# A recurrent attention and feed-forward kernel on one core: the last two tasks' products regrouped by output block, the count of the range check loaded ahead of them

## The chip, the cores and the metric

The kernel runs on one core of a Trainium2 chip. A core has TensorE (PE, matrix products into PSUM), VectorE (DVE), ScalarE (ACT), GpSimd (POOL) and SyncE (SP), each with an instruction queue of its own that runs in order; transfers are issued from the queues of SP, ACT and POOL. The metric is the time of one execution on the device in microseconds, the median of several runs.

## The reference

A recurrent attention (4 batches, 8 heads, 768 steps, head dimension 48) is followed by a feed-forward network with a gelu:

```python
for t in range(S):
    cur = einsum('bhd,bhe->bhde', u * k[t], v[t])
    y[t] = einsum('bhd,bhde->bhe', r[t], state + cur)
    state = w[t][..., None] * state + einsum('bhd,bhe->bhde', k[t], v[t])
h = x @ w_in            # x: y as 3072 tokens x 384; w_in: 384 x 2048
g = h / (1 + exp(-1.702 * h))
out = g @ w_out         # 2048 x 384
```

## The kernel before

**Attention.** The 3072 tokens are cut into 24 chunks of 128 (six chunks per batch, `CB` = 6). chunk(t) turns the recurrence within a chunk into small matmuls with running products of the decay w. load(t) fetches a chunk's inputs from SP's queue. From chunk 6 (`t >= CB`) on, half of the head pairs lie with their two heads swapped between the row halves; so when t is CB, load also fetches the u masks a second time into `hm`, in three transfers: the unswapped half of the pairs (line 169) and the swapped half in two pieces (line 171, `SWAPPED`). The first WHOLE = 8 chunks use these masks in the product `ps_d` (line 326); for a chunk from CB on it takes the second copy for all four pairs.

**Feed-forward.** The chunks form six groups of four. A task (group, first chunk, last chunk, f) does for one block f of 128 hidden units: first_product (9 matmuls x by w_in into `ph`, each value as a high and a low part, so three products per block of inputs, lines 438 to 440), gelu (two ACT operations and one VectorE operation that make the high part `gh` and the low part `gl`, lines 449 to 452) and second_product (for each of the NM = 3 blocks of 128 outputs three matmuls into `po[m]`: woh by gh, wol by gh, woh by gl, lines 465 to 467). There are 106 tasks, numbered 0 to 105; the last 16 are those of the last group, each 512 tokens wide. The three `po` tiles take one PSUM bank each and collect all 16 blocks f. store (lines 470 to 475) scales each `po[m]` on ACT into `ob` and sends it out from SP's queue, 256 KB per block.

**Order.** Everything of both parts is issued inside `tc.manual_schedule()`: the written order holds on each engine. The ramp is a list of tokens (RAMP, such as `l6` for a piece of load(6)); after it rest() yields per step j: first product j (`g`), gelu j (`h`), and second product j - LAG (`y`), LAG = 2, with the pieces of attention between. At the end of the list j runs to 107: the first product and gelu of task 104, the second product of 102, first product and gelu of 105, second products of 103, 104 and 105, and the last store.

**The range check.** While attention and weights pass through, ACT collects sums of squares and of magnitudes in `acc`. At the end (lines 570 to 581, outside the ordered region, where a planner places the operations) VectorE compares them with two limits (line 571) and adds the results (573), TensorE sums over the partitions (575, a product with one column), VectorE casts the sum to an integer in `acc` (577), and every engine loads it into a register (`nc.values_load`, 580). With `tc.If(n < full)` (581) a slow general path would follow if a limit had been passed. With these inputs it does not, so every engine branches over it; line 680 is the program's end.

Of the kernel before, what the change touches and what calls it, by code (L numbers as in the profile page):

```python
# [9 lines left out]
F32 = mybir.dt.float32  # L10
F32R = mybir.dt.float32r
BF16 = mybir.dt.bfloat16
I32 = mybir.dt.int32
U32 = mybir.dt.uint32
AF = mybir.ActivationFunctionType
ALU = mybir.AluOpType
# [78 lines left out]
def rwkv_ffn_kernel(ctx: ExitStack, tc, wkr, vp, vrk, ub, w_in, w_out, masks, vt, uc, out):  # L95
# [59 lines left out]
    def load(t):  # L155

        n = NP * CW + 1
        a, v = wkr_t[t % 2], v_t[t % 3]
        loaded[t] = [a, v]
        if t == 0:  # L160
            nc.sync.dma_start(a[ROWS, 0:n], wkr[t, :, 0:n])
            yield
            A.dma_start(a[ROWS, n:], wkr[t, :, n:])
        elif t < CB:
            nc.sync.dma_start(a[ROWS], wkr[t])
        else:
            if t == CB:
                m = 2 + 2 * HALF
                nc.sync.dma_start(hm[ROWS, 2 + H : H + m], masks[:, 2:m])
                for dst, rows in SWAPPED:  # L170
                    nc.sync.dma_start(hm[dst, H + m :], masks[rows, m:])
            kr, kr_in = (x.rearrange("r (i q c) -> r i q c", i=2, q=2) for x in (a[:, n:], wkr[t, :, n:]))
            cut = 1 + HALF * CW
            nc.sync.dma_start(a[ROWS, 0:cut], wkr[t, :, 0:cut])
            for dst, rows in SWAPPED:
                nc.sync.dma_start(a[dst, cut:n], wkr[t, rows, cut:n])
            nc.sync.dma_start(kr[ROWS, :, 0], kr_in[:, :, 0])
            for dst, rows in SWAPPED:
                nc.sync.dma_start(kr[dst, :, 1], kr_in[rows, :, 1])
        yield  # L180
        nc.sync.dma_start(v[:, OFF:], vrk[t, :, 0:DM])
        if t >= WHOLE:
            rk = pools["late"].tile([P, 2 * DM], F32, tag="rk", name="rk_t")
            nc.sync.dma_start(rk, vrk[t, :, DM:])
            loaded[t].append(rk)
        yield
# [70 lines left out]
    def bank(name):  # L257

        i = free.pop(0)
        x = ps_a.tile([P, WIDE], F32, tag=f"bank{i}", name=name)  # L260
        held[id(x)] = i, x
        while cold:
            for _ in range(cold.pop()):
                T.matmul(x.rearrange("p (n c) -> p n c", c=P), warm, warm_b, start=True, stop=True)
        return x
# [10 lines left out]
    def chunk(t):  # L276
# [45 lines left out]
        if t < WHOLE:  # L322
            got = bank("ps_d")
            ps_d = by_p(got, 2)
            for p in range(NP):
                T.matmul(ps_d[:, p], rk[:, p], u_heads[:, int(t >= CB), p], start=True, stop=True)  # L326
        yield
        if t < WHOLE:
            A.copy(s, got[:, 0:H])
# [125 lines left out]
    def second_product(j, task):  # L455
        i, c0, c1, f = task
        gh, gl = parts.pop(j)
        first = i not in po
        if first:
            po[i] = [ps_o.tile([P, WIDE], F32, tag=f"po{m}", name=f"po{m}") for m in range(NM)]  # L460
        for m in range(NM):
            ms = slice(m * P, (m + 1) * P)
            o = po[i][m][:, c0 * C : c1 * C]

            T.matmul(o, woh[:, f, ms], gh, start=first, stop=False, skip_group_check=True)  # L465
            T.matmul(o, wol[:, f, ms], gh, start=False, stop=False, skip_group_check=True)  # L466
            T.matmul(o, woh[:, f, ms], gl, start=False, stop=f == NF - 1, skip_group_check=True)  # L467

    def store(i, start, N):

        for m, o in enumerate(po.pop(i)):
            ob = pools["late"].tile([P, WIDE], F32, tag="ob", name="ob", bufs=3)[:, 0:N]
            A.activation(ob, o[:, 0:N], AF.Copy, scale=1.0 / W_SCALE)
            nc.sync.dma_start(out[m, :, bass.ds(start, N)], ob)
        xs.pop(i)

    def new_x(i):

        return (mo if i % 2 == 0 else pools["late"]).tile([P, 2, NP, WIDE], F32R, tag="x", name="x", bufs=1)

    with tc.manual_schedule():
        early = ExitStack()
        su = early.enter_context(tc.tile_pool(name="su", bufs=1))
        where = [(i, col) for i, n in enumerate(CHUNKS) for col in range(n)]
        starts = [sum(CHUNKS[:i]) for i in range(len(CHUNKS))]
        last = {}
        for j, task in enumerate(TASKS):
            last[task[0]] = j
        running, told = {}, {}

        def piece(kind, i):

            if (kind, i) not in running:
                running[kind, i] = {
                    "l": load, "a": chunk, "m": measures.get, "w": lambda i: convert(i, su, False)
                }[kind](i)
            next(running[kind, i])

        def do(token):
            kind, i = token[0], int(token[1:] or 0)  # L500
            told[token] = told.get(token, 0) + 1
            if kind in "lamw":
                piece(kind, i)
                if kind == "w" and all(told.get(f"w{n}") == 4 for n in range(2 * NL)):
                    early.close()
                    pools["late"] = fast.enter_context(tc.tile_pool(name="late", bufs=2))

                    pools["late"].tile([P, GAP], F32, tag="gap", name="gap", bufs=1)
            elif kind == "f":
                fetch(i, su)  # L510
            elif kind == "x":
                group, col = where[i]
                if i == 1:
                    fill_x(xs[group], 0, 2 * C)
                elif i == 3:
                    fill_x(xs[group], 2 * C, 4 * C)
                elif col == CHUNKS[group] - 1:
                    fill_x(xs[group], 0, (col + 1) * C)
            elif kind == "d":
                cold.append(i)  # L520
            elif kind == "u":
                nc.sync.dma_start(u_sb, ub)
            elif kind == "M":
                nc.sync.dma_start(hm[ROWS, 0 : 2 + H], masks)
            elif kind == "g":
                first_product(i, TASKS[i])
            elif kind == "h":
                gelu(i, TASKS[i])
            elif kind == "y":
                second_product(i, TASKS[i])  # L530
                group = TASKS[i][0]
                if i == last[group]:
                    store(group, starts[group] * C, CHUNKS[group] * C)

        def rest():

            begins = []
            for t, (i, col) in enumerate(where):
                n = len([x for x in TASKS if x[0] == i - 1])
                begins.append(last.get(i - 1, -1) + 1 - BEFORE - round((CHUNKS[i] - 1 - col) * n / CHUNKS[i]))  # L540
            left = []
            for t, begin in enumerate(begins):
                ramp = dict(told)
                for kind, step, half, rank in PARTS:
                    token = f"{kind}{t + 2 * (kind == 'l')}"
                    if kind == "l" and t + 2 >= NT:
                        continue
                    if ramp.get(token, 0):
                        ramp[token] -= 1
                    else:  # L550
                        left.append((step + begin, half, rank, token))
            left.sort(key=lambda x: x[:3])
            for j in range(FIRST, len(TASKS) + LAG):
                for post in range(3):
                    if post and j < len(TASKS):
                        yield f"{'gh'[post - 1]}{j}"
                    while left and left[0][:2] <= (j, post):
                        yield left.pop(0)[3]
                if j - LAG >= 0 and f"y{j - LAG}" not in told:
                    yield f"y{j - LAG}"  # L560

        for token in RAMP.split():
            do(token)
        for token in rest():
            do(token)
# [1 line left out]

    for x, limit in ((acc[:, 0 : 2 * NT], LIMIT), (acc[:, 2 * NT :], W_MAX)):  # L570
        V.tensor_single_scalar(x, x, limit, op=ALU.is_lt)
    oks = at.tile([P, 1], F32, tag="s", name="oks", bufs=2)
    V.tensor_reduce(oks, acc, axis=AX.X, op=ALU.add)
    ps = bank("ps_n")[0:1, 0:1]
    T.matmul(ps, oks, oks, start=True, stop=True)
    cnt = acc[0:1, 0:1].bitcast(I32)
    V.tensor_copy(cnt, ps)
    fast.close()
    full = P * acc.shape[1] ** 2
    n = nc.values_load(cnt, min_val=0, max_val=full)  # L580
    with tc.If(n < full):
        with tc.tile_pool(name="wp", bufs=2) as wp:
            for i in range(2 * NL):
                fetch(i, wp)
# [100 lines left out]
```

## Time and profile before

| | us |
|---|---|
| median of 3 runs | 511.07 (511.02 to 513.05) |
| profiled execution | 512.25 |
| its span in the trace | 510.5 |

| engine | busy, us | share |
|---|---|---|
| PE (matmul) | 490.8 | 96% |
| PEld (weight load, beside PE) | 407.7 | 80% |
| DVE | 296.8 | 58% |
| ACT | 249.8 | 49% |
| POOL | 13.7 | 3% |

A row of the trace's view in order of time gives start, duration, engine, line, operation, output and inputs with shapes, and in brackets the idle time before it with what ended it. In the view of one line the durations stand as minimum/median/maximum in ns, then the first and last start. SPq, PEldq and so on are instructions of an engine's queue (branches, semaphore waits, register loads, issues of transfers) that do not count as busy. Matmul durations overlap: the distance between starts is what one costs.

### The profile page before, as it was taken

To read this page: it belongs to the slowest core of one execution; us is meant where nothing else is said; L and a number is where in the kernel's file an instruction comes from. 1 tells how busy PE (TensorE), PEld (TensorE's weight loads), DVE (VectorE), ACT (ScalarE), POOL (GpSimd) and SP (SyncE) were. 2 spreads that over 40 slices of the span, in tenths; PEclk is the share of its full clock that TensorE was granted. 3 is DMA by queue.
4 is the path that set the end of the run, shared out by engine and by line. 5 is a ranking of instruction groups with operands and counts; after the bars stand their busy time and mean duration, and the time that the engine had idled before them with its cause. 6 is when DMAs were issued, how large, how long until landed. Compare 5 with 4: busy or idle time off the path is not lost.

```text
span 510.5 us, 11971 instructions
## 1 busy us (share of the span) xinstructions
PE 490.8 (96%) x5065; PEld 407.7 (80%) x5065; DVE 296.8 (58%) x507; ACT 249.8 (49%) x532; POOL 13.7 (3%) x45
## 2 busy tenths in 40 slices
PE   7788999999999999999999999999999999999994
PEld 3567999987888888888888888888888878888883
DVE  8899999787777762656556555555655521111110
ACT  4887989856726453352542543452552432322221
POOL 2010100000100010000001000001000000000000
PEclk9998899999999999999999999999999999999999
DMA  8988665034641532042204062204040001100001
GB/s 211 261 251 233 195 185 158 17 88 133 173 125 31 172 82 60 1 157 63 79 2 121 5 193 83 68 1 125 16 142 1 1 1 31 63 0 2 0 2 68
DMA packets 26830, 45.94 MB, mean 90 GB/s; under 512 B 4096, under 2 KB 17856, under 8 KB 26768
## 3 DMA queue, kind: packets, MB, share of 16 engines
q1 hardware_dynamic: 25984, 43.52, 29.9%
q0 software_dynamic: 672, 1.18, 1.2%
q8 instruction: 42, 0.69, 0.6%
q10 hardware_dynamic: 112, 0.39, 0.2%
q14 instruction: 20, 0.16, 0.1%
HBM read 38.00 MB, written 4.72 MB: 84 GB/s over the span
## 4 chain that ended last, share of the span: by engine, by line
PE 89%; DMA 5%; DVE 3%; ACT 1%; issue 1%; SPq 0%; DVEq 0%; ACTq 0%
PE po L465 14%; PE ph L438 13%; PE po L466 13%; PE po L467 13%; PE ph L439 13%; PE ph L440 13%; DMA wkr_t<-in_wkr 3%; PE ps_y L396 3%; PE ps_y L383 3%; PE ps_u L360 2%; PE ps_u L356 2%; DMA st<-in_w_in 2%; PE ps_t L306 2%; PE ps_d L326 1%; DVE lp L288 0%
## 5 line engine op out<-in xcount | busy, mean ns | idle before, releaser
L452 DVE TENSOR_TENSOR gl<-gf,gh 128x512 fp32r<-128x512 f32 (+1 forms) x106 | 67.9, 641 | 156.6 <-ACT gf L450 155.4
L449 ACT ACTIVATE gh<-ph 128x512 fp32r<-128x512 f32 (+1 forms) x106 | 59.2, 558 | 197.5 <-PE ph L440 177.8
L438 PE MATMUL ph<-x,wih 128*128 128x512 f32 (+1 forms) x318 | 119.8, 377 | 1.4 <-DMA x<-x 1.4
L465 PE MATMUL po<-gh,woh 128*128 128x512 f32 (+1 forms) x318 | 120.6, 379 | 0.0
L466 PE MATMUL po<-gh,wol 128*128 128x512 f32 (+1 forms) x318 | 118.2, 372 | 0.0
L467 PE MATMUL po<-gl,woh 128*128 128x512 f32 (+1 forms) x318 | 118.2, 372 | 0.0
L440 PE MATMUL ph<-x,wil 128*128 128x512 f32 (+1 forms) x318 | 117.4, 369 | 0.0
L439 PE MATMUL ph<-x,wih 128*128 128x512 f32 (+1 forms) x318 | 117.4, 369 | 0.0
L438 PEld LDWEIGHTS ph<-x,wih 128*128 128x128 f32 x318 | 59.9, 188 | 12.2 <-ACT junk L236 1.9
L465 PEld LDWEIGHTS po<-gh,woh 128*128 128x128 f32 x318 | 60.5, 190 | 10.8
L467 PEld LDWEIGHTS po<-gl,woh 128*128 128x128 f32 x318 | 60.6, 190 | 10.5 <-DVE gl L452 0.2
L466 PEld LDWEIGHTS po<-gh,wol 128*128 128x128 f32 x318 | 60.6, 191 | 9.5
L440 PEld LDWEIGHTS ph<-x,wil 128*128 128x128 f32 x318 | 59.9, 188 | 10.3
L439 PEld LDWEIGHTS ph<-x,wih 128*128 128x128 f32 x318 | 60.0, 189 | 9.4
L450 ACT ACTIVATE gf<-ph 128x512 f32<-128x512 f32 (+1 forms) x106 | 58.8, 555 | 2.7 <-DVE gl L452 2.6
L236 ACT ACTIVATE junk<-lp 112x1032 bf16<-112x1032 f32 x24 | 25.6, 1066 | 12.6 <-DVE lp L293 12.6
L299 DVE TENSOR_TENSOR kq<-wkr_t,lp 112x1024 f32<-112x1024 f32 x24 | 29.3, 1222 | 2.6 <-PE ps_y L396 1.6
L288 DVE TENSOR_TENSOR_SCAN lp<-wkr_t,d1r 112x516 f32<-112x516 f32 x24 | 29.4, 1225 | 1.7 <-DMA wkr_t<-in_wkr 1.7
L293 DVE TENSOR_TENSOR_SCAN lp<-wkr_t,d1f 112x516 f32<-112x516 f32 x24 | 29.6, 1231 | 0.7
L396 PE MATMUL ps_y<-kq,mid 64*64 64x64 f32 (+3 forms) x384 | 24.6, 223 | 3.6 <-DVE mid L406 1.4
L236 ACT ACTIVATE junk<-kq 112x1024 bf16<-112x1024 f32 x24 | 25.4, 1059 | 0.2
L396 PEld LDWEIGHTS ps_y<-kq,mid 64*64 64x64 f32 (+3 forms) x384 | 19.6, 130 | 5.6 <-DVE mid L406 2.1
(76 smaller groups left out, 475.1 us busy)
## 6 DMA issues: line engine op xcount, KB each, us to landing
st<-in_w_out SPq DMA_DIRECT2D x6, 1024.0 KB, 7.5
rk_t<-in_vrk SPq DMA_DIRECT2D x16, 384.0 KB, 3.5
st<-in_w_in SPq DMA_DIRECT2D x6, 896.0 KB, 8.4
v_t<-in_vrk SPq DMA_DIRECT2D x24, 192.0 KB, 2.8
out_t<-ob SPq DMA_DIRECT2D x18, 256.0 KB, 2.5
wkr_t<-in_wkr SPq DMA_DIRECT2D x18, 192.0 KB, 2.6
wkr_t<-in_wkr SPq DMA_DIRECT2D x36, 96.0 KB, 2.3
wkr_t<-in_wkr SPq DMA_DIRECT2D x5, 577.9 KB, 5.8
```

The source lines that it names most:

```text
L236: A.activation(junk[:, 0 : x.shape[1]], x, AF.Square, accum_out=acc[0:R2, i : i + 1])
L293: V.tensor_tensor_scan(pm, w0, d1f.rearrange("r p c -> r (p c)"), 0.0, op0=ALU.mult, op1=ALU.add)
L396: T.matmul(ps[b][head(h), p], from_[head(half), p * D + OFF * h : p * D + HB], qf[head(half), p, blocks[b]], start=False, stop=p == PAIRS[ ...
L438: T.matmul(ph, h_, xs[i][:, 0, c, cs], start=c == 0, stop=False)
L439: T.matmul(ph, h_, xs[i][:, 1, c, cs], start=False, stop=False)
L440: T.matmul(ph, l_, xs[i][:, 0, c, cs], start=False, stop=c == NM - 1)
L449: A.activation(gh, ph, AF.Gelu_apprx_sigmoid, scale=1.0 / W_SCALE)
L450: A.activation(gf, ph, AF.Gelu_apprx_sigmoid, scale=1.0 / W_SCALE)
L452: V.tensor_tensor(gl, gf, gh.bitcast(F32), op=ALU.subtract)
L465: T.matmul(o, woh[:, f, ms], gh, start=first, stop=False, skip_group_check=True)
L466: T.matmul(o, wol[:, f, ms], gh, start=False, stop=False, skip_group_check=True)
L467: T.matmul(o, woh[:, f, ms], gl, start=False, stop=f == NF - 1, skip_group_check=True)
```

## The change

Three parts.

1. In load(6) the transfer of the unswapped masks is dropped, and one of the two swapped pieces is issued from POOL's queue instead of SP's. The product `ps_d` takes the second copy for the swapped pairs alone.
2. The check's four operations move from behind the ordered region into it (judge), ahead of the second product of task 102 and behind gelu 104. The register load moves ahead of the last products; the branch stays where it was.
3. The second products of tasks 104 and 105 and the last store become finish(105): block by block, for each m both tasks' three matmuls, then scaling and store. The last block (m = 2) is cut into two halves of 256 tokens: six matmuls, scaling on ACT and a 128 KB store from ACT's queue for the first, six matmuls, scaling on VectorE and a 128 KB store from SP's queue for the second.

```diff
             if t == CB:
                 m = 2 + 2 * HALF
-                nc.sync.dma_start(hm[ROWS, 2 + H : H + m], masks[:, 2:m])
-                for dst, rows in SWAPPED:
-                    nc.sync.dma_start(hm[dst, H + m :], masks[rows, m:])
+                for q, (dst, rows) in zip((G, nc.sync), SWAPPED):
+                    q.dma_start(hm[dst, H + m :], masks[rows, m:])
...
-                T.matmul(ps_d[:, p], rk[:, p], u_heads[:, int(t >= CB), p], start=True, stop=True)
+                T.matmul(ps_d[:, p], rk[:, p], u_heads[:, int(t >= CB and p >= HALF), p], start=True, stop=True)
...
+    def finish(j):
+        i, c0, c1, _ = TASKS[j]
+        start, half = starts[i] * C, (c1 - c0) * C // 2
+        both = [(TASKS[q][3], *parts.pop(q)) for q in (j - 1, j)]
+        for m, o in enumerate(po.pop(i)):
+            ms = slice(m * P, (m + 1) * P)
+            ob = pools["late"].tile([P, WIDE], F32, tag="ob", name="ob", bufs=3)
+            cuts = (0, half, 2 * half) if m == NM - 1 else (0, 2 * half)
+            for n, (a, b) in enumerate(zip(cuts, cuts[1:])):
+                for f, gh, gl in both:
+                    for w, g in ((woh, gh), (wol, gh), (woh, gl)):
+                        done = f == NF - 1 and g is gl
+                        T.matmul(o[:, a:b], w[:, f, ms], g[:, a:b], start=False, stop=done, skip_group_check=True)
+                if n == 0:
+                    A.activation(ob[:, a:b], o[:, a:b], AF.Copy, scale=1.0 / W_SCALE)
+                else:
+                    V.tensor_single_scalar(ob[:, a:b], o[:, a:b], 1.0 / W_SCALE, op=ALU.mult)
+                q = A if m == NM - 1 and n == 0 else nc.sync
+                q.dma_start(out[m, :, start + a : start + b], ob[:, a:b])
...
             elif kind == "y":
-                second_product(i, TASKS[i])
                 group = TASKS[i][0]
-                if i == last[group]:
+                if i == len(TASKS) - 4:
+                    judge()
+                if i == len(TASKS) - 1:
+                    bad.append(nc.values_load(cnt, min_val=0, max_val=full) < full)
+                    finish(i)
+                elif i < len(TASKS) - 2:
+                    second_product(i, TASKS[i])
+                if i == last[group] and i < len(TASKS) - 1:
                     store(group, starts[group] * C, CHUNKS[group] * C)
+
+        def judge():
+            for x, limit in ((acc[:, 0 : 2 * NT], LIMIT), (acc[:, 2 * NT :], W_MAX)):
+                V.tensor_single_scalar(x, x, limit, op=ALU.is_lt)
+            oks = at.tile([P, 1], F32, tag="s", name="oks", bufs=2)
+            V.tensor_reduce(oks, acc, axis=AX.X, op=ALU.add)
+            got = bank("ps_n")
+            ps = got[0:1, 0:1]
+            T.matmul(ps, oks, oks, start=True, stop=True)
+            V.tensor_copy(cnt, ps)
+            release(got)
...
-    for x, limit in ((acc[:, 0 : 2 * NT], LIMIT), (acc[:, 2 * NT :], W_MAX)):
-        V.tensor_single_scalar(x, x, limit, op=ALU.is_lt)
-    oks = at.tile([P, 1], F32, tag="s", name="oks", bufs=2)
-    V.tensor_reduce(oks, acc, axis=AX.X, op=ALU.add)
-    ps = bank("ps_n")[0:1, 0:1]
-    T.matmul(ps, oks, oks, start=True, stop=True)
-    cnt = acc[0:1, 0:1].bitcast(I32)
-    V.tensor_copy(cnt, ps)
     fast.close()
-    full = P * acc.shape[1] ** 2
-    n = nc.values_load(cnt, min_val=0, max_val=full)
-    with tc.If(n < full):
+    with tc.If(bad[0]):
```

More of the change, by code (lines that the diff above doesn't have):

```diff
@@ L475, in store @@
         xs.pop(i)
+    def finish(j):
[17 more added lines that the diff above has]
+                q.dma_start(out[m, :, start + a : start + b], ob[:, a:b])
+        xs.pop(i)
     def new_x(i):
@@ L529, in do @@
             elif kind == "y":
-                second_product(i, TASKS[i])
                 group = TASKS[i][0]
-                if i == last[group]:
-                    store(group, starts[group] * C, CHUNKS[group] * C)
+                if i == len(TASKS) - 4:
[6 more added lines that the diff above has]
+                if i == last[group] and i < len(TASKS) - 1:
+                    store(group, starts[group] * C, CHUNKS[group] * C)
+        def judge():
[8 more added lines that the diff above has]
+            release(got)
+        cnt = acc[0:1, 0:1].bitcast(I32)
+        full = P * acc.shape[1] ** 2
+        bad = []
         def rest():
```

## The prediction

> **What bounds the kernel now.** I read the page's chain first, then the trace in order of time from 490 us on, then the queues' own instructions there.
>
> ```profile
> PE 89%; DMA 5%; DVE 3%; ACT 1%; issue 1%; SPq 0%; DVEq 0%; ACTq 0%
> ```
>
> TensorE carries 89% of the chain that ended last, so whatever stops PE in the last 20 us is paid in full, and so is whatever comes after PE's last matmul. The last tasks, in order of time:
>
> ```profile
> 492.27 0.39 PE L440 MATMUL ph<-x,wil 128*128 128x512 f32 x1
> ...
> 492.72 0.39 PE L466 MATMUL po<-gh,wol 128*128 128x512 f32 x1
> ...
> 493.81 0.69 DVE L452 TENSOR_TENSOR gl<-gf,gh 128x512 fp32r<-128x512 f32 x1 [3.39 <-ACT gf L450]
> ...
> 498.61 0.39 PE L465 MATMUL po<-gh,woh 128*128 128x512 f32 x1
> ...
> 500.74 0.09 PEld L575 LDWEIGHTS ps_n<-oks 128*1 128x1 f32 x2 [0.35 <-issue]
> ...
> 500.87 0.50 PE L465 MATMUL po<-gh,woh 128*128 128x512 f32 x1
> ...
> 501.20 0.39 PE L466 MATMUL po<-gh,wol 128*128 128x512 f32 x1
> ...
> 501.86 1.99 ACT L473 ACTIVATE ob<-po 128x512 f32<-128x512 f32 x3 [4.00 <-PE po L467]
> ...
> 502.82 0.40 PE L467 MATMUL po<-gl,woh 128*128 128x512 f32 x1
> ```
>
> 492.27 is the last matmul of task 104's first product; task 102's second product follows at once (its second matmul at 492.72, so a 512-column matmul every 0.227 us). Task 104's gl is written by VectorE from 493.81 to 494.50. 498.61 opens task 104's second product, 500.87 task 105's. The count's matmul (L575) lies between those two. The third activation ends at 501.86 + 1.99 = 503.85. After that:
>
> ```profile
> 503.24 1.37 SPq L474 DMA_DIRECT2D out_t<-ob  x1
> 504.71 0.37 SPq L474 DMA_DIRECT2D out_t<-ob  x1
> DMA to landing us min/median/max: 3.1/3.1/3.1
> L581 SPq COMPARE_BRANCH  x1: 45/45/45, 505.1 to 505.1; - x1
> L581 SPq EVENT_SEMAPHORE  x8: 17/17/17, 508.3 to 508.9; - x8
> L581 PEldq COMPARE_BRANCH  x1: 3637/3637/3637, 501.9 to 501.9; - x1
> L581 DVEq COMPARE_BRANCH  x1: 72/72/72, 501.8 to 501.8; - x1
> L581 DVEq EVENT_SEMAPHORE  x1: 21/21/21, 504.7 to 504.7; - x1
> ```
>
> The last store is ready at 503.85 but SP issues it at 504.71, because the second store's issue takes 1.37. It lands 3.1 later, at 507.8. SP, which takes the branch over the general path at 505.1, runs its next instruction only at 508.3, half a us after the landing: **SP's jump of about 3.15 sets the end, not the store.** VectorE's jump takes 2.8 (501.9 to 504.7), TensorE's branch 3.64. From 508.3 to the end at 510.5 SP counts off semaphores and the last barrier runs. Why did one issue take 1.37?
>
> ```profile
> q8 instruction: 1, 0.02, 5.9%
> 144.47 1.31 SPq L181 DMA_DIRECT2D v_t<-in_vrk  x1
> q8 instruction: 1, 0.02, 6.2%
> ```
>
> The first row is the DMA view of 502.90 to 504.25: one instruction fetch on q8. The second and third show it elsewhere: an SP issue that began inside such a fetch (window 144.2 to 145.4) lasted until 145.78, 0.38 after that window; in the tail it lasted until 504.61, 0.36 after. The tail's fetch follows TensorE's branch (501.9) by one us. So TensorE's jump holds up an SP issue that falls into its fetch.
>
> **The change, part by part.**
>
> *The count's place.* judge() is issued after task 104's gelu and before task 102's second product, and this region keeps the written order on each engine. VectorE gets its three operations behind gl104, TensorE gets the count's matmul ahead of task 102, and behind that matmul wait all of TensorE's later products. Today the three run early, in holes:
>
> ```profile
> L571 DVE TENSOR_SCALAR acc<-acc x2: 164/172/179, 91.2 to 401.5; 128x12 f32<-128x12 f32 x1, 128x48 f32<-128x48 f32 x1
> L573 DVE TENSOR_REDUCE oks<-acc x1: 203/203/203, 402.0 to 402.0; 128x1 f32<-128x60 f32 x1
> 125.81 0.15 ACT L406 COPY mid<-ps_y 1x1 f32<-1x1 f32 x1 [0.36 <-PE ps_y L396]
> 126.01 0.13 PEld L396 LDWEIGHTS ps_y<-kq,mid 64*64 64x64 f32 x1 [0.42 <-ACT mid L406]
> ```
>
> gl104 ends at 494.50; 0.179 + 0.164 + 0.203 = 0.55 makes 495.05; TensorE wakes 0.05 after the operation it waits for (125.96 to 126.01). From the count's weight load to the second full matmul behind it are 501.20 - 500.74 = 0.46. So task 102's second matmul moves from 492.72 to 495.56: **+2.84**, which nothing hides, since all of TensorE's remaining work is behind it and gelu 105 moves along. On VectorE the count's cast and gl105 are queued behind, but gl105's inputs come later by the same 2.84. Bounds: 2.6 if the VectorE operations overlap, 3.1 with a further gap at each. The stall's cover would be VectorE's idle 3.39 ahead of gl104, but the operations are queued behind gl104, not in it.
>
> *The register load* stands before the last products. TensorE's costs nothing:
>
> ```profile
> L580 PEldq TENSOR_LOAD <-acc x1: 485/485/485, 501.3 to 501.3; - x1
> ```
>
> It ran at 501.3 while matmuls went on until after 502.82: the queue covers its 0.49, and it would cost that if the queue ran dry. ACT, SP and VectorE are idle at its new place.
>
> *The tail, in the old clock (without the 2.84).* The count's matmul is gone from it: task 105's second matmul would come ten pitches after 498.61, at 500.89 instead of 501.20, a gain of 0.32. Blocks 0 and 1 take twelve matmuls, 498.61 to 501.34. Block 2 is twelve matmuls of 256 columns:
>
> ```profile
> 57.92 0.12 PE ph L439
> ...
> 62.00 0.12 PE ph L440
> ...
> L449 ACT ACTIVATE gh<-ph 128x256 fp32r<-128x256 f32 x20 | 7.7, 384 | 1.6 <-PE po L466 1.6
> L406 DVE COPY mid<-ps_y x16: 145/146/147, 144.1 to 418.3; 1x1 f32<-1x1 f32 x16
> L367 DVE TENSOR_TENSOR mid<-ps_u,sf x20: 357/358/359, 19.3 to 401.7; 112x192 f32<-112x192 f32 x20
> ```
>
> 35 such matmuls from 57.92 on keep 0.12, so the halves cost 12 x 0.12 = 1.44 against 1.36. First half: last matmul 501.94. Today 0.43 pass from the last matmul's start to ACT's (502.82 to 503.25), 0.11 less with 256 columns: ACT starts at 502.26, takes 0.38, ends 502.64 and issues its store in the shade. Second half: it writes the same bank (po2) that ACT is reading. Does TensorE wait? No row has just this; the nearest:
>
> ```profile
> 44.67 0.67 PE ps_u L356 x23
> 45.34 0.61 PE ps_u L360 x27
> ...
> 45.98 0.37 DVE mid L367
> ```
>
> L367 reads only what L356 wrote, yet it starts behind L360, which writes other columns of the same bank. So I take it that banks are kept apart as a whole, in the other direction too. Between nothing and 0.75, I take the wait: TensorE resumes at 502.69, loses 0.10 restarting, its sixth matmul is at 503.39, VectorE starts at 503.71. Its operation was never run at this shape; from 0.146 at one element and 0.358 at 192, 256 give 0.43 (bounds 0.33 to 0.5). SP can issue at about 504.15.
>
> [...]
>
> *The issue and the jump.* TensorE sends its last instruction between 502.69 and 503.39 and then branches; its fetch starts one us later and lasts about 1.3, so it covers roughly 503.9 to 505.25. SP's last issue at 504.15 begins inside it and ends 0.37 after it, at 505.6, branch 505.6: **+0.45** against today's 505.14. SP's jump, between 2.8 (VectorE's) and 3.15 (its own), taken in the middle: **-0.18**. The 128 KB landing stays under it (504.71's 256 KB needed 3.1).
>
> *The ramp.*
>
> ```profile
> L169 SPq DMA_DIRECT2D hm<-in_masks x1: 1174/1174/1174, 59.7 to 59.7; - x1
> L171 SPq DMA_DIRECT2D hm<-in_masks x2: 420/424/428, 60.9 to 61.4; - x2
> 110.63 0.47 PE ps_d L326 x5
> ```
>
> SP loses L169 and one L171 (1.17 + 0.42), POOL gains one DMA. The masks are first used by chunk 6's ps_d at 110.6, nearly 50 us later, and TensorE is busy around 60. I take 0 and keep 0.3 both ways.
>
> Sum: 2.84 + 0.45 - 0.18 = +3.1. The profiled execution took 512.25, span 510.5, so 1.7 lie outside the span; its time stands 1.2 above the median 511.07. The sum is a difference of spans and I add it to the median: **514.2**.
>
> **The rivals.**
> 1. *The last issue misses the fetch* (TensorE's branch goes out later or VectorE ends sooner; 0.2 us decide). Issue 504.15 to 504.53, branch 504.59, -0.55: 2.84 - 0.55 - 0.18 = +2.1, **513.2**.
> 2. *No wait on the bank.* The second half runs on at 502.06 to 502.66, VectorE 502.98 to 503.41, SP 503.45 to 503.82, branch 503.86, -1.28: +1.4, **512.5**. For it speaks that the halves share no bytes; against it L367.
> 3. *No stall, not slower.* If VectorE's three operations came ahead of gl104, in its idle 3.39, the sums would be ready before 492.44 and TensorE would not wait. Then only the tail counts: between -1.28 - 0.18 = -1.5 (**509.6**) and +0.3 (**511.3**). For it: the same operations are placed early today. Against: today they stand behind the ordered region, now within it.
> 4. *The clock drops in the stall.*
>
> ```profile
> 46.00:47.00 1.00, 0.00 (x0) 0.00 (x0) 0.90 (x3) 1.00 (x5) 0.00 (x0) 1.00 0.67 125
> 47.00:48.00 1.00, 0.36 (x14) 0.40 (x18) 1.00 (x3) 0.77 (x2) 0.00 (x0) 0.69 0.79 233
> 54.00:55.00 1.00, 1.00 (x9) 0.91 (x7) 1.00 (x3) 1.00 (x2) 1.00 (x3) 0.90 0.29 96
> ```
>
> A pause of under 2 us at 46, behind small matmuls, dropped the clock to 0.5 from 47.4 to 54.2. Seven us at half speed would add 3.4: **517.6**. Against it: here full-size matmuls stand on both sides of the pause. [...]
>
> **How the numbers follow.** Forecast 0.48, rival 1 0.25, rival 2 0.14, rival 3 0.06, rival 4 0.07. From 512.3 to 515.0 the range holds the forecast and rival 1 with their bounds (0.70) and most of rival 2. A measurement of this kernel tells about 0.5% (2.6 us) from no change: 513.6 is the upper edge. Most of the forecast, a quarter of rival 1 and rival 4 lie above: 0.54. Rivals 2 and 3 and the rest of the others lie within: 0.43. Faster needs rival 3 and a better tail than computed: 0.03.
>
> **What would show it.** Right: an idle of TensorE of about 2.7 us ahead of the count's matmul, released by VectorE's reduce; 256-column matmuls at 0.12; a pause of about 0.75 between the halves, released by ACT; SP's last issue above 1 us; about 3 us from SP's branch to its next instruction. Wrong: the count's matmul without idle time ahead of it (rival 3), or no pause between the halves (rival 2), or a granted clock of 0.5 after the stall (rival 4). The forecast falls as a whole if the last matmul does not come about 3 us later than today.

## The result and the profile after

| | before | after |
|---|---|---|
| median of 13 runs each, us | 512.29 | 515.16 (513.21 to 519.07) |
| ratio after / before | | 1.0066 (95%: 1.0042 to 1.0089) |
| profiled execution, us | 512.25 | 514.21 |
| its span, us | 510.5 | 512.5 |

The changed kernel is slower by the ratio's 0.66%, about 3.4 us. One run of before took 2748.78 us; without it the median of before is 512.04 and the two medians lie 3.1 apart. The forecast was 3.1 us slower. The time itself, 515.16, lies 0.16 above the upper end of the range, 515.0: the median of before is 1.0 above that of the 3 runs to which the forecast was added. That the difference came out nearly right is luck: two errors of the sum cancelled, as will be seen.

The page's chain of the changed kernel, which answers to the first row of the prediction:

```profile
PE 88%; DMA 4%; DVE 3%; ACT 3%; issue 1%; SPq 0%; POOL 0%; DVEq 0%; ACTq 0%; POOLq 0%
```

TensorE still carries it. Shares this coarse (1% is 5 us) don't show a change of 3 us; it has to be looked for in the stretch of the change, in order of time:

```profile
491.07 0.39 PE L439 MATMUL ph<-x,wil 128*128 128x512 f32 x1
...
492.61 0.69 DVE L451 TENSOR_TENSOR gl<-gf,gh 128x512 fp32r<-128x512 f32 x1 [3.38 <-ACT gf L449]
493.22 0.26 DVE L567 TENSOR_SCALAR acc<-acc 128x48 f32<-128x48 f32 x2
493.51 0.22 DVE L569 TENSOR_REDUCE oks<-acc 128x1 f32<-128x60 f32 x1
493.78 0.09 PEld L572 LDWEIGHTS ps_n<-oks 128*1 128x1 f32 x2 [2.75 <-DVE oks L569]
493.90 0.79 PE L464 MATMUL po<-gh,woh 128*128 128x512 f32 x1
494.50 0.63 PE L465 MATMUL po<-gh,wol 128*128 128x512 f32 x1
494.92 0.63 PE L466 MATMUL po<-gl,woh 128*128 128x512 f32 x1
...
497.31 0.40 PE L466 MATMUL po<-gl,woh 128*128 128x512 f32 x1
...
504.95 0.28 PE L491 MATMUL po<-gl,woh 128*128 128x256 f32 x1
505.70 0.38 PE L491 MATMUL po<-gh,woh 128*128 128x256 f32 x1 [0.47 <-ACT ob L493]
506.39 0.28 PE L491 MATMUL po<-gl,woh 128*128 128x256 f32 x1
506.77 0.43 DVE L495 TENSOR_SCALAR ob<-po 128x256 f32<-128x256 f32 x1 [5.16 <-PE po L491]
507.22 0.33 SPq L497 DMA_DIRECT2D out_t<-ob  x1
```

Three things are to be seen. The weight load of the count's product waits 2.75 behind VectorE's reduce. The products behind it last 0.63 and start 0.42 apart, not 0.23. And the two halves of the last block are parted by a wait on ACT's scaling. The second is the clock; the windows of one us (length, busy time of PE, PEld, DVE, ACT and POOL with counts, granted clock, DMA share, GB/s) show it:

```profile
492.00:493.00 1.00, 0.00 (x0) 0.00 (x0) 0.39 (x1) 0.58 (x2) 0.00 (x0) 1.00 0.00 0
493.00:494.00 1.00, 0.21 (x3) 0.18 (x3) 0.70 (x4) 0.00 (x0) 0.00 (x0) 0.83 0.00 0
494.00:495.00 1.00, 1.00 (x3) 0.81 (x4) 0.15 (x1) 0.00 (x0) 0.00 (x0) 0.50 0.00 0
...
496.00:497.00 1.00, 1.00 (x3) 0.77 (x3) 0.00 (x0) 0.00 (x0) 0.00 (x0) 0.50 0.00 0
497.00:498.00 1.00, 1.00 (x5) 0.77 (x4) 0.00 (x0) 0.00 (x0) 0.00 (x0) 0.96 0.00 0
```

The granted clock fell to 0.50 from 493.67 to 497.08, so for 3.41 us.

**Where the 3.2 us of the end came from.** The spans can't be compared from their start, because the changed kernel's trace is already 1.12 ahead at the first gelu (33.96 against 35.08), before the first instruction of the change, which comes at about 60 us. So I measure from the gelu of task 100 (start of its second ACT operation, gf), where the two still run alike, in three legs: to gf of task 105, from there to the start of the last matmul, and from there to the end of the span. The rows that group these ACT operations of the last six tasks give the first leg to a tenth, as the distance of first and last start; before, then after:

```profile
L450 ACT ACTIVATE gf<-ph x6: 594/594/594, 476.9 to 497.3; 128x512 f32<-128x512 f32 x6
```

```profile
L449 ACT ACTIVATE gf<-ph x6: 591/593/593, 475.7 to 500.3; 128x512 f32<-128x512 f32 x6
```

| us, from the trace | gf 100 to gf 105 | to the last matmul | to the end | sum |
|---|---|---|---|---|
| before | 20.40 | 5.55 | 7.71 | 33.66 |
| after | 24.62 | 6.10 | 6.10 | 36.83 |

The first leg grew by 4.22, the stall and the slow clock together. The other two shrank by 1.06, where the prediction had +0.27. The net is 3.17, and less the 1.20 by which this execution was ahead at task 100 (475.67 against 476.87) it is the 2.0 between the spans.

### The profile page after: what moved, and what is told of

Its sections match the earlier page's. It is cut to its first block, busy times and chain, and to the rows that moved or that the text cites. A ratio compares the mean times of both kernels' runs of the same rounds, so it can differ in the third digit from the quotient of the medians.

```text
span 512.5 us, 11987 instructions
## 1 busy us (share of the span) xinstructions
PE 492.1 (96%) x5071; PEld 409.4 (80%) x5071; DVE 297.3 (58%) x508; ACT 249.7 (49%) x532; POOL 14.3 (3%) x46
## 4 chain that ended last, share of the span: by engine, by line
PE 88%; DMA 4%; DVE 3%; ACT 3%; issue 1%; SPq 0%; POOL 0%; DVEq 0%; ACTq 0%; POOLq 0%
PE po L464 13%; PE ph L437 13%; PE ph L439 12%; PE ph L438 12%; PE po L466 12%; PE po L465 12%; DMA st<-in_w_in 3%; PE ps_y L382 3%; PE ps_y L395 3%; PE ps_u L359 2%; PE ps_u L355 2%; PE ps_t L305 2%; PE po L491 1%; PE ps_d L325 1%; DMA x<-x 0%
## 5 line engine op out<-in xcount | busy, mean ns | idle before, releaser
L464 PE MATMUL po<-gh,woh 128*128 128x512 f32 (+1 forms) x312 | 119.0, 381 | 0.0
L465 PE MATMUL po<-gh,wol 128*128 128x512 f32 (+1 forms) x312 | 116.5, 373 | 0.0
L466 PE MATMUL po<-gl,woh 128*128 128x512 f32 (+1 forms) x312 | 116.4, 373 | 0.0
```

## The experiments

**Theory.** The loss is the stall of TensorE behind gelu 104 (2.75 us) and the half clock that the stall can bring (1.5 us); the new tail gives back about one us, by its order of blocks, which frees SP's issues of their hold; cutting the last block in two gives nothing. **Rivals:** the new tail itself costs time and the stall is only a part; the half clock has a cause of its own and would come without a pause of the array; the early register load, not the order of blocks, is what shortened the tail; the ramp's edit moved the whole execution.

Each kernel differs from the changed kernel by the edit shown, save the one that starts from before. The ratio is to the kernel before, run in the same batch on the same chip.

### The changed kernel again

> The change as it is, on the same chip and beside the same runs of the kernel before as the next three. Theory A (wait for the count 2.75, half clock in about six runs of ten, tail about 1 shorter): +2.5 to +3.4 against the kernel before, TensorE idle 2.7 ahead of the count's matmul. A rival D (much of the difference of the first comparison was the state of its chip): under +2.

Measured 514.82 (9 runs), ratio 1.0053 (1.0028 to 1.0079), 3.1 above before: as expected. Legs 24.75, 6.11, 6.21, sum 37.07. The half clock is there again, though it starts later, from 495.64 to 499.05:

```profile
493.00:494.00 1.00, 0.00 (x0) 0.00 (x0) 0.97 (x4) 0.00 (x0) 0.00 (x0) 1.00 0.00 0
...
495.00:496.00 1.00, 1.00 (x6) 0.76 (x5) 0.00 (x0) 0.00 (x0) 0.00 (x0) 0.82 0.00 0
496.00:497.00 1.00, 1.00 (x4) 0.81 (x3) 0.00 (x0) 0.00 (x0) 0.00 (x0) 0.50 0.00 0
```

TensorE was idle up to 494.15, yet ran at full clock for 1.5 us after that before the clock fell. So the drop does not come when the array stops; the account of the prediction below comes back to when it comes.

### The sums ahead of the gelu

```diff
             elif kind == "h":
+                if i == len(TASKS) - 2:
+                    sums()
                 gelu(i, TASKS[i])
```

sums() holds VectorE's three operations of judge(); the count's product and its cast stay in judge().

> The change, with the three VectorE operations of the count issued ahead of task 104's gelu instead of behind it. Theory A (the loss is TensorE's wait for the count, 2.75 us, and the half clock that this wait brings, 1.7 us per window; the new tail itself gains about 1): no idle of TensorE ahead of the count's matmul, clock 1.0 until the end, 1.0 us shorter than the kernel before. Rival B (the loss sits in the tail: the halves, their wait on the bank and the two queues): the wait goes but the time stays above the kernel before, +0.5 to +1.5. Rival C (the clock drops by itself near the end, not through the wait): half clock again, about +0.7.

Measured 511.93, ratio 0.9994 (0.9968 to 1.002); legs 20.76, 6.10, 6.23, sum 33.09. The views of waits and of time, from 490 us on:

```profile
PEld ps_n L578 <- issue: 0.4, 1, 0.4
```

```profile
492.58 0.09 PEld L578 LDWEIGHTS ps_n<-oks 128*1 128x1 f32 x2 [0.35 <-issue]
...
493.81 0.69 DVE L451 TENSOR_TENSOR gl<-gf,gh 128x512 fp32r<-128x512 f32 x1 [2.96 <-ACT gf L449]
```

The count's product now runs 1.2 us before task 104's gl, its wait is 0.35, and no half clock follows. Three operations moved by a few lines take away the whole loss: the sum falls by 3.74. It is 0.57 below that of before, where 1.0 was expected, and the time is that of before (511.93 against 511.95). The first leg, 20.76, is 0.36 longer than before because the count's product now lies in it; in the kernel before it lay in the second. So of the 2.75 by which the stall lengthens the first leg, 0.36 is the product itself, and the stall proper is 2.39.

### The array kept busy through the wait

```diff
             got = bank("ps_n")
+            for _ in range(11):
+                T.matmul(got.rearrange("p (n c) -> p n c", c=P), warm, warm_b, start=True, stop=True)
             ps = got[0:1, 0:1]
```

> The change, with eleven matmuls of ones (128x512, thrown away) ahead of the count's matmul, so that TensorE waits as long but is busy. Theory A: the clock stays at 1.0 there, task 102's products keep a pitch of 0.227, and the time is 1.7 us below the change, or more where its runs show a clock under 0.985: about +1.7 against the kernel before, and its runs scatter less. Rival C: half clock as before, no gain. Rival B says nothing here but that the tail costs the same.

Measured 513.62, ratio 1.002 (0.9994 to 1.0045); legs 23.14, 6.11, 6.17, sum 35.42. The windows:

```profile
492.00:493.00 1.00, 1.00 (x7) 0.43 (x5) 0.47 (x1) 0.49 (x2) 0.00 (x0) 1.00 0.00 0
...
494.00:495.00 1.00, 1.00 (x5) 0.83 (x6) 0.07 (x1) 0.00 (x0) 0.00 (x0) 1.00 0.06 16
```

The products of task 102 are as late as in the changed kernel, but the array never rests and the clock stays at 1.00. The first leg is 1.48 shorter than the changed kernel's: that is the price of the half clock, separated from that of the wait. The time is 1.67 above before, as expected, and the runs lie closer together (512.75 to 514.96, against 513.21 to 519.07 in the changed kernel). That the busy array is what kept the clock up is not shown by this trace alone: the next two kernels kept it with an idle array.

### The last block whole

```diff
-            cuts = (0, half, 2 * half) if m == NM - 1 else (0, 2 * half)
+            cuts = (0, 2 * half)
...
-                q = A if m == NM - 1 and n == 0 else nc.sync
-                q.dma_start(out[m, :, start + a : start + b], ob[:, a:b])
+                nc.sync.dma_start(out[m, :, start + a : start + b], ob[:, a:b])
```

> The change, with the last block uncut: six matmuls of 512 columns, one activation, one store of 256 KB from SP's queue. Theory A: the halves' pause of 0.7 goes; SP's last issue comes 0.6 earlier after the last matmul, the larger store lands about 0.5 later after its issue, and the jump of 2.6 to 3.1 sets the end: 0 to 0.6 us below the change. Rival B: well below it, 1.5 or more. If the halves do help, 0.3 or more above it.

Measured 513.99, ratio 1.003 (1.0001 to 1.0059); legs 23.15, 5.20, 6.87, sum 35.22. Its waits and windows:

```profile
PEld ps_n L571 <- DVE oks L568: 2.8, 1, 2.8
```

```profile
494.00:495.00 1.00, 0.00 (x0) 0.00 (x0) 0.96 (x4) 0.00 (x0) 0.00 (x0) 1.00 0.00 0
...
496.00:497.00 1.00, 1.00 (x6) 0.81 (x5) 0.00 (x0) 0.00 (x0) 0.00 (x0) 1.00 0.00 0
497.00:498.00 1.00, 1.00 (x6) 0.82 (x5) 0.00 (x0) 0.00 (x0) 0.00 (x0) 1.00 0.00 0
```

```profile
L449 ACT ACTIVATE gf<-ph x6: 592/593/593, 477.1 to 500.2; 128x512 f32<-128x512 f32 x6
```

The same stall of 2.8, and this time no half clock. So the drop does not follow from the stall alone. The first leg, 23.15, agrees with that of the kernel with the busy array: the stall without the clock costs 2.75 over before. The time is 2.0 above before, so about 1 below the change (3.1 above before in the repeat), more than the 0 to 0.6 expected; in the traces the sum is 1.61 below, of which 1.47 is the half clock that this execution did not have.

### The old tail behind the same stall

```diff
-                    finish(i)
-                elif i < len(TASKS) - 2:
-                    second_product(i, TASKS[i])
-                if i == last[group] and i < len(TASKS) - 1:
+                second_product(i, TASKS[i])
+                if i == last[group]:
                     store(group, starts[group] * C, CHUNKS[group] * C)
```

> The count's new place and its early load alone: tasks 104 and 105 and the last store as in the kernel before. Theory A: the wait and the half clock as in the change, and the old tail without the count's matmul in it (-0.3): +4.1 against the kernel before, about 0.7 above the change. Rival B: most of the loss is gone, below +2.

Measured 516.22, ratio 1.0072 (1.0042 to 1.0101); legs 23.15, 5.20, 8.65, sum 37.00. The slowest of all, again without the half clock in its profiled execution. Its last leg is 1.8 longer than that of the whole block. SP's second store is one row of the view of time:

```profile
505.25 1.90 SPq L473 DMA_DIRECT2D out_t<-ob  x1
```

It was held for 1.90 where such an issue otherwise takes 0.33, and the last store waited behind it. The expected +4.1 was hit (516.22 against 511.95), but in this trace not by what was expected: there is no half clock in it, and one issue was held longer (1.90 against 1.37 before). In that, the hit is luck.

### Early sums with the whole block, and with the old tail

The edits of the above, put together.

> The count's sums ahead of gelu 104, and the last block uncut, stored from SP's queue. Theory A: no wait, no half clock near the end; from task 100's second gelu operation to the end 33.0 in the trace (before 33.66, with the halves 33.09), about -0.6 against the kernel before; the halves are worth nothing. If the halves help, 0.3 or more above the run with them.

Measured 511.32, ratio 0.9992 (0.997 to 1.0014); legs 20.76, 5.20, 6.71, sum 32.67.

> The count's sums ahead of gelu 104 and the early load, with the old tail. Theory A: the same time as the kernel before (0 +- 0.4): the second store follows the first within 0.8, begins inside TensorE's fetch and is held until 0.37 after it. Rival E (what shortened the tail is the early load, not the order by blocks): -0.6, as with finish.

Measured 511.81, ratio 1.001 (0.9991 to 1.003); legs 20.76, 5.20, 7.51, sum 33.47.

The ratios can't part the two, and both are within 0.5% of before; the legs can, with care. With the old tail the count is loaded early all the same, and the last leg is 7.51 against 7.71 before (and 8.23 in the next kernel, whose tail is that of before): the early load is not what shortened the tail by 1.6. Written block by block it is 6.71, so that order is worth 0.8 here; behind the stall it was 1.8 (6.87 against 8.65). From the last matmul to SP's branch, without the jump, it is 1.45 against 2.40, and 1.45 against 3.08 behind the stall; SP's longest issue accounts for nearly all of that (0.33 against 1.22 and 1.90).

Against the first of these kernels, the one with early sums and two halves reads 33.09: the cut costs 0.9 ahead of the last matmul and returns 0.5 behind it, a loss of 0.4. In the pair behind the stall it returned 0.8 (6.10 against 6.87), a loss of 0.1. The last leg contains SP's jump, which differs between executions by more than these losses, so the cut's net is only known to be no clear gain. Up to SP's branch it returns 0.2 in both pairs (1.23 against 1.45); the rest lies in SP's jumps, shorter in these traces with the cut (2.6 to 2.8 against 3.0 to 3.2).

### The ramp's edit alone

Before, with only the masks' transfers and line 326 of the change.

```diff
-                nc.sync.dma_start(hm[ROWS, 2 + H : H + m], masks[:, 2:m])
-                for dst, rows in SWAPPED:
-                    nc.sync.dma_start(hm[dst, H + m :], masks[rows, m:])
+                for q, (dst, rows) in zip((G, nc.sync), SWAPPED):
+                    q.dma_start(hm[dst, H + m :], masks[rows, m:])
...
-                T.matmul(ps_d[:, p], rk[:, p], u_heads[:, int(t >= CB), p], start=True, stop=True)
+                T.matmul(ps_d[:, p], rk[:, p], u_heads[:, int(t >= CB and p >= HALF), p], start=True, stop=True)
```

> The kernel before with the masks' part of the change alone. Theory A: no difference that can be measured (0 +- 0.3); in the trace the distance from task 4's to task 100's second gelu operation is that of the kernel before within 0.3. Rival F (one transfer less on SP in the ramp brings the 1.2 us by which the changed kernel's profile ran ahead): -1 or more, seen between tasks 4 and 12.

Measured 512.38, ratio 1.0008 (0.9983 to 1.0033). From the gelu of task 4 to that of task 100 it took 423.76 against 423.40 before and 423.33 in the changed kernel. Nothing that can be measured, either way. Nor is the changed kernel's lead at the start the edit's work as far as the traces tell: the gelu of task 4 comes at 53.47 before and between 51.88 and 54.13 in the eleven traces with the edit. The legs are 20.40, 5.55, 8.23. The instructions of the tail are those of before, and yet the last leg is 0.5 longer, most of it in SP's jump (3.60 against 3.17): so much can a last leg differ without any change to the tail.

### The last store from ACT's queue

The kernel with early sums and the whole block, with one more line:

```diff
+                q = A if m == NM - 1 else nc.sync
```

> As the one two above (sums early, last block uncut) with the last store issued from ACT's queue, so that SP jumps 1.3 earlier, behind the second block's store. If SP's jump sets the end: 0.7 to 1.2 less than with SP's store, about -1.5 against the kernel before, and SP waits for the last landing. If the landing or TensorE's jump (4.1) sets it: no gain, 0 to -0.3.

Measured 510.32, ratio 0.9976 (0.9955 to 0.9997): the one kernel of the study that is faster than before, by 0.24%, with an interval that ends just below 1. Legs 20.76, 5.20, 5.71, sum 31.67. In order of time, and then the branch's line:

```profile
500.23 1.69 SPq L497 DMA_DIRECT2D out_t<-ob  x2
...
502.33 0.60 ACT L493 ACTIVATE ob<-po 128x512 f32<-128x512 f32 x1 [0.76 <-PE po L491]
502.96 0.38 ACTq L497 DMA_DIRECT2D out_t<-ob  x1
```

```profile
L622 SPq EVENT_SEMAPHORE  x8: 17/17/17, 504.9 to 505.9; - x8
L622 SPq COMPARE_BRANCH  x1: 45/45/45, 502.0 to 502.0; - x1
```

SP, free of the last store, takes the branch at 502.0, before ACT has even scaled the last block, and its jump of 2.9 runs beside the last store. It comes out of it at 504.9 and counts semaphores until 505.9, just after the last store has landed (505.83). Here, for the first time, the landing and not the jump sets the end. It is worth 1.0 against the kernel without this line.

### The old tail with its stores spaced

The kernel with early sums and the old tail, with the middle store on ACT's queue, so that SP's issues lie further apart:

```diff
-            nc.sync.dma_start(out[m, :, bass.ds(start, N)], ob)
+            (A if m == 1 and i == len(CHUNKS) - 1 else nc.sync).dma_start(out[m, :, bass.ds(start, N)], ob)
```

> Sums ahead of gelu 104 and the old tail, with the second block's store of the last group issued from ACT's queue, so that SP's two issues lie 1.4 apart. If an SP issue is held only when it follows another within a us (theory A): SP's last issue takes 0.33 although it begins inside or near the fetch, and from SP's last issue's start to its branch pass 0.4 instead of 1.3; the third activation comes 0.1 to 0.4 later behind ACT's own issue, and the end comes 0.5 to 0.9 earlier after the last matmul than with all three on SP. If the fetch holds any issue (the prediction's rule): SP's last issue takes 0.8 or more.

Measured 511.86, ratio 0.9995 (0.9972 to 1.0019); legs 20.76, 5.20, 6.98, sum 32.94. SP's last issue, and the DMA view of 504.62 to 505.66 (queue, kind: packets, MB, share):

```profile
504.78 0.33 SPq L473 DMA_DIRECT2D out_t<-ob  x1
```

```profile
q8 instruction: 1, 0.02, 6.1%
```

The issue began inside a fetch and took 0.33, as the first of the two cases expected. With the middle store on SP's queue (the kernel with early sums and the old tail) SP's last issue meets a fetch too (503.32 to 504.67), 0.75 after the issue before it, and it is held:

```profile
503.61 1.22 SPq L473 DMA_DIRECT2D out_t<-ob  x1
```

## Why the prediction was right in size and wrong in its sum

**The count's place: right.** +2.84 was forecast, by VectorE's three operations behind gl104. The legs give 2.75 (23.15 against 20.40), the same in the two kernels with the stall and a full clock, 0.36 of it the count's product, which moved here out of the second leg; the row shows the weight load waiting for the reduce, as forecast. Rival 3, no stall, falls. With the sums ahead of the gelu the stall is gone, so it is the place of the operations, not the operations, that costs.

**The clock: a step that failed, a term that the sum lacked.** The sum put the half clock at nothing; rival 4 was given 0.07, on the argument that full-size matmuls stand on both sides of the pause. They did, and the clock fell to 0.50 all the same, which the prediction had named as a sign of being wrong. The first leg of the changed kernel is 1.47 longer than that of the same stall at full clock (24.62 against 23.15), 1.60 in the repeat: some 3.41 us at half speed. The price of rival 4, 3.4, was too dear, as it took the seven us seen in the ramp, which were two beats of 3.41; half of one beat is 1.7, the figure in the expectations. Whether it comes seems to depend on the phase: in all traces the clock changes on a beat of 3.41 us (in the changed kernel's its changes lie 6.83, 440.32, 3.41 and 13.65 apart: 2, 129, 1 and 4 beats). The pause of the array is 2.33 in four traces. Carrying the beat back from the trace's last change of clock, 2.21 of the pause (after) and 1.93 (the repeat) lay within one beat and the clock dropped; with the whole block the larger share was 1.22, with the old tail 1.51, and it did not. After the last matmul the array rests for good, which gives more cases. From 470 us on, the twelve traces hold 14 beats at whose end the clock dropped, all with 1.93 or more idle, and 13 with 0.40 to 1.81 idle at whose end it stayed. So from 470 us on the two kinds part between 1.81 and 1.93. The ramp does not keep to that: in the kernel before, among small matmuls, a beat with 1.69 idle (43.96 to 47.38) ended in a drop. And no kernel was made that shifts the phase on purpose, so this is a reading that fits the cases from 470 us on, not a test of it.

**The halves and the bank: right.** Shifted by 3.02 (501.63 against 498.61), the prediction puts the first half's last matmul at 504.96, the second half's first at 505.71, its last at 506.41 and VectorE's start at 506.73; measured 504.95, 505.70, 506.39 and 506.77. The 0.10 for the restart is there too: the second matmul of that half starts 0.22 after the first (505.92), the others 0.12 apart. The wait stands in the view of waits of the changed kernel, so rival 2 falls:

```profile
PEld po L491 <- ACT ob L493: 0.7, 1, 0.7
```

That banks are kept apart as a whole was inferred from one row, L367; the runs show the wait of these two halves, 0.7 in the four traces with such halves.

**SP's last issue: the other step that failed.** "SP's last issue at 504.15 begins inside it and ends 0.37 after it", +0.45. It did begin inside the fetch (507.22, in 507.02 to 508.48) and was not held: it took 0.33, and SP's branch came at 507.62, 0.54 earlier than today's in the shifted clock instead of 0.45 later. The fetch is in the DMA view of 507.0 to 508.5 of the changed kernel:

```profile
q8 instruction: 1, 0.02, 6.1%
```

The fetch was placed rightly; the rule that an issue in a fetch is held was wrong. The spaced stores point to what else it needs. Over the twelve traces 155 issues of SP began inside a fetch on q8 (from 0.05 before its start to 0.3 before its end). 91 were held until about 0.37 after its end; every one of them began 0.75 or less after SP's issue before it. Of the 64 that were not held, 53 began 1.36 or more after it; the other 11, all at one place of the ramp, came 0.68 after it and right at the fetch's start. No issue in a fetch lies between 0.75 and 1.36, so where the hold ends is not known, nor why a close issue is held. The two rows of the prediction were both of the close kind. Block by block, the stores lie 1.36 apart or more, and the issue of 1.37 that today's tail pays is back to 0.33.

**The jump: small.** "-0.18" was -0.53: SP's branch at 507.62, its next instruction at 510.26, so 2.64 against 3.17 (505.14 to 508.31). Over all traces the same jump of SP took 2.6 to 3.6, and no run shows what sets it. Its rows after:

```profile
L616 SPq EVENT_SEMAPHORE  x8: 17/17/17, 510.3 to 510.8; - x8
...
L616 SPq COMPARE_BRANCH  x1: 45/45/45, 507.6 to 507.6; - x1
```

That the jump and not the landing sets the end was right (the last store landed at 509.95, before 510.26), and is what the last store on ACT's queue turns to a gain.

**The sum.** Forecast 2.84 + 0.45 - 0.18 = 3.1; measured from task 100 on 2.75 + 1.47 - 1.06 = 3.16, where the -1.06 is the count's product gone from the second leg (-0.35), the cut (+0.90) and what follows the last matmul (-1.61). The tail's 1.3 that were too dear (+0.27 forecast, -1.06 measured) and the clock's 1.5 that were left out cancelled by luck. In the tail it is the price of rival 1 (-0.55), though not its condition, as the issue did begin inside the fetch; in the middle it is rival 4. No single case of the prediction held both. The ramp at 0 was right within what can be measured. With the difference nearly right, what put the time outside the range was the base: the forecast was added to the median of 3 runs of before, 511.07, and more runs have it at 512.04 (12) and, beside the experiments, at 511.65 to 511.95.

## What to carry to other kernels

An operation that is moved into a hand-written order waits behind everything written before it on its engine: put it ahead of the long operation, in the engine's idle time, not behind it, or the bottleneck pays for the whole chain (2.75 us here, 0.36 with the operations ahead). A pause of TensorE may cost a second time (here one of 2.33 us cost 1.5 to 1.6 more in two of four traces); price it with a chance, not with nothing. At the end of a kernel, look at which engine's jump ends last and take the last transfer away from that engine's queue (1.0 us here).

## What the runs showed of the hardware

- Of the SP issues that began inside an instruction fetch, 91 were held until about 0.37 after it, all 0.75 or less after SP's issue before; none of the 53 that came 1.36 or more after it was held, nor were 11 that came 0.68 after it, at the fetch's start.
- A pause of the array of 2.33 us, between full-size matmuls, halved the clock for 3.41 us in two executions of one kernel, and did not in two other kernels with the same pause; from 470 us on, 1.93 idle of a beat of 3.41 dropped it and 1.81 did not; in the ramp of the kernel before, 1.69 did.
- In the kernel as built, matmuls into one half of a PSUM bank waited 0.7 for ACT's reading of the other half; no run shows what happens without that wait. Cutting the block cost 0.9 ahead of the last matmul and won 0.5 to 0.8 behind it.
- The jump over an untaken body of code takes SP 2.6 to 3.6 us; for ACT it was 0.47 in the changed kernel.
